# An adaLN block on one core: modulation products untied from the zero products, and a new written order

## The chip, the cores and the metric

The kernel runs on one core of one Trainium2 chip. The core has five engines with a queue each: TensorE (PE; its weight loads are shown apart as PEld), VectorE (DVE), ScalarE (ACT), GpSimd (POOL), and SyncE (SP), which here only issues DMAs. Each works off its own list of instructions in order and waits at semaphores for the others. The metric is the device time of one execution in microseconds (us), the median of several runs. A time, a start or an end without further words is in us from the start of the profiled span.

## What is computed

A transformer block with adaptive layer norm, for one sequence of 2048 tokens of width 640, in bf16:

```python
mod = (silu(c) @ w_mod).reshape(1, 6, 1, -1)
sa, ca, ga, sb, cb, gb = (mod[:, i] for i in range(6))
h = layernorm(x) * (1 + ca) + sa
q, k, v = split(h @ wqkv)                 # 32 heads of width 20
scores = q @ k^T * 20 ** -0.5             # causal, a window of 256 keys
x = x + ga * ((softmax(scores) @ v) @ wo)
h = layernorm(x) * (1 + cb) + sb
x = x + gb * ((sigmoid(h @ w_gate) * (h @ w_up)) @ w_down)   # inner width 1536
```

`silu(c) @ w_mod` gives the six modulation vectors. The first two, `sa` and `ca`, are needed before anything can be projected to q, k and v.

## The kernel before

**Order.** `build` does not issue instructions. It makes a list of 2021 operations (`A(...)`, that is `Prog.op`), each with the engines that may run it, what it reads and writes, and the tiles it occupies. `Prog.schedule` then walks through `PLAN`, a list of 2021 numbers written out by hand or by a search outside the file. A number `code` means: operation `code // 5` comes next, on engine `code % 5` of (pe, act, dve, pool, sp). So `PLAN` settles both the engine of an operation that has a choice and the order on each engine. `SLOTS` gives, in the order in which tiles are first used, which buffer of its pool each tile takes. Between engines nothing is ordered by `PLAN` itself: `Prog.emit` puts semaphore waits where an operation reads what another wrote, or takes a buffer that another has to leave. One more rule is in `schedule`: a POOL operation that stands in `PLAN` behind a DVE operation marked `port=True` waits for the last such one to end.

**Work.** The tokens go in 8 chunks of 256 (two blocks of 128 each). For a chunk: the layer norm statistics on DVE, a power on POOL, the normalised x on DVE or POOL, a transposition (on PE for chunks 0 and 1, by DMA later), the modulation by `sa` and `ca`, the projections, scores in sets of one PSUM tile S with an exponential on ACT (80 in all), masks on POOL, the product with v on PE ("pvs", two for each chunk), a normalisation on DVE, the output projection, the second norm and the gated MLP. As there is one S tile, a set of scores waits until the exponential of the set before has read it. The rest of PE's work is put between the sets.

**The start.** This is the part that the change names. Operation numbers are those of the kernel before.

- SP loads x of chunk 1 (27), the second half of chunk 0 (17), its first half (16), five pieces of `w_mod` for `sa` and `ca` (18 to 22, into the tile `wd`, which is free then), then wq, wk and so on.
- `zeros(n)` makes one PE operation of n products of a zero tile (each 128x512, into a bank of S that nobody reads). `HEAT` makes seven such operations (41 to 47, 11 products) ahead of the modulation products. `REHEAT` makes one after each of the five modulation operations: 51, 53, 55, 57 and 59.
- The modulation of the first norm, `fnA`: five operations on PE (50, 52, 54, 56, 58, called modA), one for each 128 rows of `w_mod`, of ten products of 64 columns each. Each has `extra=wprev`, that is, it also depends on the `zeros` operation made before it, and each `zeros` depends on the modA before it. So the twelve stand in one fixed order in any `PLAN`. A DVE copy (60) then brings the result to the tile mA, which every modulation of the first norm reads.
- Norm of chunk 0: statistics 67 to 69 (first half of the rows) and 70 to 72 (second half), powers 73 to 76 on POOL, normalised halves 77 and 78 on DVE, transpositions 79, 81 (of 77) and 88, 90 (of 78) on PE, copies out of PSUM 80, 82, 89, 91, modulations 83 to 87 and 92 to 96. Chunk 1: statistics 149 to 154, powers 155 and 156, normalised halves 157 and 158, transpositions 159 to 167.
- The first projections of q are 120 and 121, which read 92 to 96. The first set of scores is 308.

**Later operations that are spoken of.** 225 is the second group of modulation products ("modt"), which needs the last piece of `w_mod` (load 34, issued by SP). 220 to 224 scale `wo`, 370 to 381 scale `wd` by a gate vector ("wos", "wds"; DVE or POOL). 558, 645, 792 and 875 are the pvs of chunks 1 (first, second) and 2 (first, second). 303 to 307 are modulations of chunk 3's hT, 300 is a normalised half of chunk 3 on POOL.

**Lines of the profile.** L621 zero products, L634 full-array products (all projections, MLP, transpositions and modA), L635 products in parts of the array (scores, pvs, modt), L741 and L743 statistics, L747 and L749 powers, L762 and L759 normalised x, L726 the copy to mA, L822 and L823 modulations of chunk 0, L947 masks, L981 exponentials, L1206 wds, L1272 wos, L533 loads, L664 and L665 copies out of PSUM.

## Time and profile before

| | us |
|---|---|
| median of 3 runs (lowest, highest) | 324.32 (324.31, 324.38) |
| the profiled execution's own time | 324.32 |
| its span, first to last instruction | 322.6 |
| outside the span | 1.7 |
| PE busy | 316.8 |
| ACT, DVE, POOL busy | 214.6, 199.9, 193.9 |

A row of the timeline begins with the start in us, then the duration in us, the engine, the line, the operation, the tile it writes and the tile it reads, and the number of instructions merged into the row. In brackets stands the idle time of that engine just before and what ended it. Rows of grouped lines end with the busy time, the mean duration of one instruction in ns, and the idle time before the group. PE's products overlap, so the rate is read from the starts of many (15 products of 320 columns take 2.14 us), not from the duration of one.

### The profile page before, as it was taken

Reading aid. Unit: us, or ns where it says so; the run is one execution under the profiler, and the core shown is the slowest. Engines: PE = TensorE matmul, PEld = TensorE weight load, DVE = VectorE, ACT = ScalarE, POOL = GpSimd, SP = SyncE. Lnnn points to the kernel's source line nnn. Section 1 sums busy time; section 2 is a strip of 40 time slices with the busy share of each in tenths; the row PEclk is TensorE's granted clock in tenths of the full one; section 3 lists DMA queues with packets and bytes.
Section 4 is the critical chain, followed back from the end, with each engine's and each line's share of the span. In section 5 each row is a group of like instructions: output and inputs, shape, how many; then the busy total and the mean of one; then the engine's idle time right before and its main releaser. Section 6 shows DMA issues by size and latency. Waiting matters only on the chain.

```text
span 322.6 us, 11139 instructions
## 1 busy us (share of the span) xinstructions
PE 316.8 (98%) x4766; PEld 230.9 (72%) x4766; DVE 199.9 (62%) x424; ACT 214.6 (67%) x220; POOL 193.9 (60%) x334
## 2 busy tenths in 40 slices
PE   6999999999999999999999999999999999999997
PEld 2666656577776677766787667876788777877885
DVE  6796999677585545685557454676438453485422
ACT  1489999997798787859785858684768557200320
POOL 4338679788788596969393839585672836601000
PEclk9999999999999999999999999999999999999999
DMA  7999799999912343308250211420400021012111
GB/s 231 374 332 199 198 258 206 184 273 317 210 40 41 103 92 48 62 3 130 55 114 4 35 35 48 102 43 2 122 6 4 2 43 43 2 41 43 41 43 42
DMA packets 64619, 33.61 MB, mean 104 GB/s; under 512 B 49082, under 2 KB 63034, under 8 KB 64570
## 3 DMA queue, kind: packets, MB, share of 16 engines
q1 hardware_dynamic: 63744, 31.92, 42.3%
q10 hardware_dynamic: 826, 0.98, 0.9%
q8 instruction: 37, 0.61, 0.8%
q14 instruction: 12, 0.10, 0.1%
HBM read 18.35 MB, written 2.62 MB: 65 GB/s over the span
## 4 chain that ended last, share of the span: by engine, by line
PE 89%; POOL 4%; ACT 3%; DVE 2%; DMA 1%; issue 1%; SPq 0%; ACTq 0%; DVEq 0%; POOLq 0%
PE M L634 74%; PE S L635 8%; PE M L635 7%; POOL E L947 3%; ACT E L981 2%; DMA x<-in_A_x_dram 1%; DVE x L762 1%; DVE st L741 1%; POOL st L749 1%; POOL st L747 0%; ACT QT L664 0%; DVE hT L823 0%; DVE st L743 0%; ACT hT L777 0%; SPq L533 0%
## 5 line engine op out<-in xcount | busy, mean ns | idle before, releaser
L947 POOL TENSOR_SCALAR_AFFINE_SELECT E<-E 128x256 bf16<-128x256 bf16 (+2 forms) x234 | 149.3, 667 | 52.2 <-ACT E L981 34.5
L981 ACT ACTIVATE E<-S 128x2048 bf16<-128x2048 f32 x80 | 150.2, 1878 | 42.3 <-PE S L635 41.6
L634 PE MATMUL M<-h2T,wu 128*128 128x256 bf16 x480 | 66.4, 273 | 0.0
L634 PE MATMUL M<-h2T,wg 128*128 128x256 bf16 x480 | 65.8, 273 | 0.0
L1225 DVE SCALAR_TENSOR_TENSOR hh<-sig,M 128x512 bf16<-128x512 f32 x48 | 32.4, 681 | 43.8 <-ACT sig L1223 31.6
L634 PE MATMUL M<-wd,hh 128*128 128x320 bf16 (+2 forms) x396 | 56.4, 295 | 0.0
L634 PEld LDWEIGHTS M<-h2T,wu 128*128 128x128 bf16 x480 | 45.7, 98 | 8.1 <-issue 1.6
L634 PEld LDWEIGHTS M<-h2T,wg 128*128 128x128 bf16 x480 | 45.5, 98 | 8.3 <-issue 1.5
L634 PEld LDWEIGHTS M<-wd,hh 128*128 128x128 bf16 x396 | 37.0, 98 | 14.9 <-issue 1.4
L1223 ACT ACTIVATE sig<-M 128x512 f32<-128x512 f32 x48 | 28.4, 596 | 26.1 <-PE M L634 25.0
L635 PE MATMUL S<-QT,KT 20*64 20x64 bf16 (+5 forms) x1600 | 33.3, 231 | 0.5
L1112 DVE STREAM_TRANSPOSE T<-M 128x512 f32<-128x512 f32 x32 | 21.7, 698 | 12.2 <-PE S L635 10.0
L741 DVE BATCH_NORM_STATS2 st<-x 128x6 f32<-128x320 bf16 x64 | 28.3, 477 | 1.1 <-DMA x<-in_A_x_dram 0.8
L635 PEld LDWEIGHTS S<-QT,KT 20*64 20x64 bf16 (+1 forms) x1600 | 15.2, 99 | 18.4 <-ACT E L981 9.8
L634 PE MATMUL M<-wk,hT 128*128 128x320 bf16 x160 | 28.2, 300 | 0.0
L634 PE MATMUL M<-wv,hT 128*128 128x320 bf16 x160 | 28.0, 300 | 0.0
L634 PE MATMUL M<-wo,oT 128*128 128x320 bf16 x160 | 26.5, 300 | 0.0
L634 PE MATMUL M<-wq,hT 128*128 128x320 bf16 x160 | 26.0, 300 | 0.2 <-DVE hT L823 0.2
L1244 DVE TENSOR_TENSOR x<-M,x 128x320 bf16<-128x320 f32 (+2 forms) x33 | 15.4, 478 | 15.1 <-PE M L634 14.5
L1179 DVE TENSOR_TENSOR x<-M,x 128x320 bf16<-128x320 f32 x32 | 15.3, 487 | 13.6 <-PE M L634 13.0
L747 POOL TENSOR_SCALAR st<-st 128x2 f32<-128x2 f32 (+1 forms) x17 | 4.0, 233 | 32.7 <-DVE st L743 31.7
L635 PEld LDWEIGHTS M<-E,V 128*32 128x32 bf16 x960 | 19.9, 97 | 4.5 <-issue 2.2
(81 smaller groups left out, 298.9 us busy)
## 6 DMA issues: line engine op xcount, KB each, us to landing
x<-in_A_x_dram SPq DMA_DIRECT2D x11, 320.0 KB, 3.6
wd<-in_w_mod_dram SPq DMA_DIRECT2D x6, 320.0 KB, 5.0
wd<-in_B_w_down_dram SPq DMA_DIRECT2D x4, 480.0 KB, 5.3
out_dram<-x SPq DMA_DIRECT2D x5, 320.0 KB, 2.6
wg<-in_B_w_gate_dram SPq DMA_DIRECT2D x2, 576.0 KB, 6.9
wu<-in_B_w_up_dram SPq DMA_DIRECT2D x2, 576.0 KB, 6.2
wu<-in_w_mod_dram SPq DMA_DIRECT2D x1, 960.0 KB, 10.5
wq<-in_A_wqkv_dram SPq DMA_DIRECT2D x2, 400.0 KB, 6.7
```

What stands on the lines that cost most here:

```text
L634: return e.matmul(o, l, r, start=st, stop=sp, skip_group_check=True)
L635: return e.matmul(o, l, r, start=st, stop=sp, tile_position=tp, skip_group_check=True)
L741: A("dve", lambda e, g, bi=bi, j=j: e.bn_stats(v(bi * 12 + j * 6, 6), src[bi].ap[:, j * 320:(j + 1) * 320]), 0.48, reads=[src[bi].r()], wr ...
L747: A("pool", lambda e, g, lo=lo, w=w: e.tensor_scalar(v(28 + lo, w), var()[:, lo:lo + w], EPS, None, op0=ALU.add), 0.2, reads=[st.r(("m", b ...
L749: A("pool", lambda e, g, lo=lo, w=w: e.tensor_tensor(v(30 + lo, w), v(28 + lo, w), mhalf[:, 0:w], op=ALU.pow), 0.71, reads=[st.r(("v", lo) ...
L947: return lambda e, eng: e.affine_select(dst(), src(), pattern=pattern, compare_op=ALU.is_ge, fill=0.0, base=base, channel_multiplier=mul)
L981: A("act", lambda e, eng: e.activation(dst(), src(Sp.ap), ACT.Exp, scale=SM_SCALE), 1.876, reads=[Sp.r()], writes=[E.r()], prio=3, tag=f"e ...
L1112: A("dve", lambda e, g, h=h: e.transpose(T1.ap[:, 512 * h:512 * h + 512], X[h].ap), 0.694, reads=[X[h].r()], writes=[T1.r(h)], prio=3.5, t ...
L1179: A("dve", lambda e, g, ps=ps, bi=bi, half=half: e.tensor_tensor(x1[bi].ap[:, half * 320:half * 320 + 320], ps.ap[:, 0:320], x1[bi].ap[:, ...
L1223: A("act", lambda e, g, pg=pg, sg=sg: e.activation(sg.ap[:], pg.ap[:], ACT.Tanh, scale=0.5), c_act(512), reads=[pg.r()], writes=[sg.r()], ...
L1225: A("dve", lambda e, g, pu=pu, sg=sg, f0=f0: e.scalar_tensor_tensor(out=hh.ap[:, f0:f0 + 2, :], in0=sg.ap[:].rearrange("p (a b) -> p a b", ...
L1244: A("dve", lambda e, g, ps=ps, bi=bi, c0=c0, n=n: e.tensor_tensor(x1[bi].ap[:, c0:c0 + n], ps.ap[:, 0:n], x1[bi].ap[:, c0:c0 + n], op=ALU. ...
```

## The change

Three things. First, the modulation products no longer depend on `zeros` operations (`extra=wprev` is gone), so an order may put them elsewhere among the zero products. Second, `REHEAT` becomes (2, 1, 1, 0, 3): there is one `zeros` operation less (57), while the number of zero products stays 18, the one of 57 being issued by 59. Third, `PLAN` and `SLOTS` are new: 2020 numbers, the first 150 places searched anew and the others moved a little.

```diff
-REHEAT = (2, 1, 1, 1, 2)
+REHEAT = (2, 1, 1, 0, 3)
...
         if kt:
-            zeros(REHEAT[kt - 1], oA[-1:])
-        oA.append(A("pe", fnA, MW / 2400.0 * 10, reads=[Rm[0][kt], R_silubc], writes=[psA.r()], prio=0, lat=0.2, tag="modA", extra=wprev))
+            if REHEAT[kt - 1]:
+                zeros(REHEAT[kt - 1], oA[-1:])
+        oA.append(A("pe", fnA, MW / 2400.0 * 10, reads=[Rm[0][kt], R_silubc], writes=[psA.r()], prio=0, lat=0.2, tag="modA"))
```

The beginning of the old and the new `PLAN`:

```diff
-    76, 139, 89, 63, 84, 202, 94, 3, 8, 243, 38, 175, 245, 72, 182, 186, 192, 197, 99, 53, 58, 13, 33, 18, 48, 104,
-    109, 114, 357, 352, 124, 119, 129, 134, 747, 362, 378, 383, 337, 342, 392, 767, 347, 752, 762, 205, 210, 215,
...
+    243, 3, 8, 33, 76, 48, 28, 245, 38, 175, 58, 23, 202, 182, 139, 757, 205, 210, 215, 220, 225, 230, 89, 84, 94,
+    63, 186, 192, 197, 99, 332, 104, 13, 337, 342, 109, 352, 363, 347, 250, 260, 742, 368, 357, 373, 382, 400, 235,
```

Read out by engine, with the numbers of the kernel before (in the new file every operation from 58 on has a number smaller by one), the start is:

```
PE before: 35 49 41-46 88 47 90 50 51 52 53 81 54 79 55 56 57 58 59 159 167 161 120 121 163 ...
PE after:  49 35 41-46 50 52 81 47 51 79 53 54 55 88 90 56 58 59 159 161 167 120 121 163 ...
DVE before: 40 14 36 38 39 71 70 149 72 67 68 78 153 69 150 152 154 151 77 89 82 158 157 60 96 92 94 95 ...
DVE after:  40 36 152 38 39 67 68 69 71 70 149 72 77 153 150 154 151 78 158 157 60 93 96 95 168 14 85 ...
POOL before: ... 75 76 73 74 155 156 86 84 239 ...
POOL after:  ... 73 74 75 76 155 156 92 13 83 84 86 3 10 239 ...
ACT before: 15 37 91 80 93 160 162 87 ...
ACT after:  15 37 82 80 91 89 94 160 87 162 164 ...
```

SP issues the same loads in the same order up to load 29 of the modulation weights. Behind the start, 109 operations have another engine: 33 went from ACT to DVE, 31 from DVE to ACT, 27 from DVE or ACT to POOL, 12 from POOL to DVE or ACT, and 6 DMA issues between SP and ACT. The places that matter below:

```
POOL before, up to the masks of 558: ... 297 298 299 300 247 327 330 then 12 masks
POOL after,  up to the masks of 558: ... 297 298 299 245 249 327 330 300 224 221 223 then 12 masks, 307 and 305 among them
PE before: 554 342 272 278 279 282 558 474 475 471 225 566 ...
PE after:  554 278 282 279 225 558 474 475 471 486 472 499 566 ...
ACT before, between the exponentials of 554 and 558: 305 306 304 303 307
ACT after,  between the exponentials of 554 and 558: 280 215 303
POOL before, from the masks of 645 to those of 875: 24 masks, 5 wds, 2 bmodu0, 2 xh5, 4 pow5, 2 bpow1
POOL after,  from the masks of 645 to those of 875: 24 masks, 6 wds, 2 bmodu0, 2 xh5, 1 pow5, 2 pow6, 1 amodu5
```

Ahead of 792, PE does 12 steps of the MLP of chunk 0 less than before (two products of 256 columns each), and ahead of 875 it does 6 steps of k projections and 3 of the down projection less; these follow behind.

14 lines of the change are left out of this document (7 added, 7 removed), and 216 rows, old and new, of the table PLAN.

## The prediction

> **What bounds the kernel now.** I read the page first (busy shares, then the chain that ended last), then the windows by stage, then the timeline of the start and of the places where PE waits.
>
> ```profile
> PE 316.8 (98%) x4766; PEld 230.9 (72%) x4766; DVE 199.9 (62%) x424; ACT 214.6 (67%) x220; POOL 193.9 (60%) x334
> ...
> PE 89%; POOL 4%; ACT 3%; DVE 2%; DMA 1%; issue 1%; SPq 0%; ACTq 0%; DVEq 0%; POOLq 0%
> ```
>
> PE is busy for 316.8 of 322.6 us and holds 89% of the chain. It works off one list, and every projection, score and MLP product of the old list is in the new one. So the time can move in two ways only: the first useful product starts earlier or later, or PE waits more or less afterwards. The first is set by this stretch:
>
> ```profile
> 3.13 0.49 DVE L609 COPY silubc<-siluc 128x320 bf16<-128x320 bf16 x1
> ...
> 4.41 1.28 DVE L741 BATCH_NORM_STATS2 st<-x 128x6 f32<-128x320 bf16 x3 [0.78 <-DMA x<-in_A_x_dram]
> ...
> 5.88 0.23 POOL L747 TENSOR_SCALAR st<-st 128x1 f32<-128x1 f32 x1 [2.41 <-DVE st L743]
> 5.90 0.89 DVE L741 BATCH_NORM_STATS2 st<-x 128x6 f32<-128x320 bf16 x2
> ...
> 6.20 0.58 POOL L749 TENSOR_TENSOR st<-st,mhalf 128x1 f32<-128x1 f32 x1
> 6.82 0.45 DVE L762 TENSOR_SCALAR x<-x,st 128x640 bf16<-128x640 bf16 x1
> ...
> 8.56 0.28 DVE L743 BATCH_NORM_AGGREGATE st<-st 128x2 f32<-128x12 f32 x2
> ...
> 9.64 0.71 POOL L749 TENSOR_TENSOR st<-st,mhalf 128x2 f32<-128x2 f32 x1
> ...
> 10.39 0.81 DVE L762 TENSOR_SCALAR x<-x,st 128x640 bf16<-128x640 bf16 x2 [0.36 <-POOL st L749]
> ...
> 11.10 0.17 DVE L726 COPY mA<-S 128x10 f32<-128x10 f32 x1
> ...
> 12.05 0.94 PE L634 MATMUL M<-wq,hT 128*128 128x320 bf16 x5 [0.24 <-DVE hT L823]
> ...
> 12.55 0.90 POOL L823 TENSOR_SCALAR hT<-hT,mA 128x128 bf16<-128x128 bf16 x2 [2.20 <-DVE hT L823]
> ```
>
> The reader is to see that DVE hardly pauses from 4.41 to 11.27: statistics, normalised halves, and only then the copy to mA. The first projection starts at 12.05, when the modulations behind that copy are through. The modulation products on PE are not late:
>
> ```profile
> 2.72 4.44 PE L621 MATMUL S<-E 128*128 128x512 bf16 x10
> ...
> 8.12 0.59 PE L621 MATMUL S<-E 128*128 128x512 bf16 x2
> ...
> 10.60 0.45 PE L634 MATMUL S<-silubc,wd 128*128 128x64 bf16 x10
> ```
>
> The last ten end at 11.05, just ahead of the copy at 11.10. So the dependency that is taken out costs little by itself; what counts is the new order.
>
> **The start, step by step.** The new DVE list takes the first half of chunk 0 (16) before the second (17). The loads are issued as before, and they land so:
>
> ```profile
> 1.30 0.45 SPq L533 DMA_DIRECT2D x<-in_A_x_dram  x1
> ...
> DMA to landing us min/median/max: 3.1/3.1/3.1
> ```
>
> ```profile
> 1.80 0.42 SPq L533 DMA_DIRECT2D x<-in_A_x_dram  x1
> ...
> DMA to landing us min/median/max: 4.1/4.1/4.1
> ```
>
> The second half is there at 1.30 + 3.1 = 4.4, the first only at 1.80 + 4.1 = 5.9. Before, DVE used the time between for the second half's three statistics (4.41). In the new list only 152, siluc (38) and silubc (39) stand ahead of 67. Chunk 1 was loaded first, so 152 is done by about 4.4 and silubc by about 5.1 (0.49, and a short step before it). DVE then stands still from 5.1 to 5.9. From there: 67 and 68 until 6.8 (0.89), 69 until 7.0, three statistics in 1.2 until 8.2, 72 until 8.4. The normalised half 77 runs 8.4 to 8.8 (its power on POOL is done at 8.0). Two statistics (0.8) and two aggregates (0.28) end at 9.8. The powers 155 and 156 follow at 9.9 and end at 9.9 + 0.32 + 0.71 = 10.95; 78 hides in that time. Then 158 and 157 take 0.81, and the copy to mA starts at about 11.7 and not at 11.10. PE is ready for it: 88 and 90 follow 78 at 10.3, 56 and 58 end by 11.4.
>
> ```profile
> 2.62 0.42 POOL L554 MEMSET stg<- 128x384 bf16 x1
> ```
>
> Behind the copy (11.87) the modulation 92 now goes to POOL: 0.1 to hand over and 0.45, so projection 120 starts at 12.45 instead of 12.05: **+0.4**. POOL has four operations behind it (13, 83, 84, 86: 0.42 + 3 x 0.45) and ends at 14.2; projection 98 wants 86 at 14.35. That cover is thin: one more modulation there would cost 0.3.
>
> From 12.05 to score set 308 both lists hold the same operations. The chain shows a pause ahead of that set:
>
> ```profile
> 18.80 0.14 issue
> ```
>
> The new list puts transposition 103 one step (two products) earlier, which covers the copy 104. So 308 is late by 0.4 - 0.15 = **+0.25**. Bounds of the start: -0.35, if the first half lands as fast as the second (DVE's pause of 0.8 gone: 0.4 - 0.8 and some 0.05 elsewhere), and +0.7, if the modulations on POOL come late as well. I take +0.25, which uses the landing as the row shows it.
>
> **At the first pvs of chunk 1 (558).** In the new list POOL gets three scalings of wo, one normalised half and two modulations between the last mask of chunk 0 and those of 558; PE gets modt (225) ahead of 558.
>
> ```profile
> 33.26 3.06 POOL L947 TENSOR_SCALAR_AFFINE_SELECT E<-E 128x1024 bf16<-128x1024 bf16 x2
> 39.29 1.22 POOL L947 TENSOR_SCALAR_AFFINE_SELECT E<-E 128x512 bf16<-128x512 bf16 x2 [2.97 <-DVE wo L1272]
> 42.21 5.66 POOL L947 TENSOR_SCALAR_AFFINE_SELECT E<-E 128x1024 bf16<-128x1024 bf16 x8 [1.70 <-ACT V L664]
> 48.21 2.13 POOL L947 TENSOR_SCALAR_AFFINE_SELECT E<-E 128x1024 bf16<-128x1024 bf16 x2 [0.34 <-ACT E L981]
> ```
>
> ```profile
> L1206 POOL TENSOR_TENSOR wd<-wd,gbc 128x640 bf16<-128x640 bf16 x5 | 6.9, 1394 | 1.8 <-DVE hT L778 1.2 <-DMA wd<-in_B_w_down_dram 0.5
> L759 POOL TENSOR_SCALAR x<-x,st 128x640 bf16<-128x640 bf16 x6 | 5.2, 871 | 1.6 <-PE M L634 1.2 <-POOL st L754 0.2 <-DVE Tn L1116 0.2
> ...
> L778 POOL TENSOR_SCALAR hT<-hT,mA 128x256 bf16<-128x256 bf16 x5 | 2.8, 556 | 0.0
> ```
>
> ```profile
> 50.62 1.50 PE L635 MATMUL M<-E,V 128*32 128x256 bf16 x64
> ...
> 54.08 0.24 PE L635 MATMUL M<-hh,silubc 128*32 128x160 bf16 x4
> 54.44 0.40 PE L635 MATMUL S<-QT,KT 20*128 20x128 bf16 x16
> ```
>
> Before, POOL was free at 36.32, worked 9.0 on these masks (1.22 + 5.66 + 2.13) and idled 5.0 (2.97 + 1.70 + 0.34). The added work is 3 x 1.39 (row of wd, same shape) + 0.87 + 2 x 0.56 = 6.2, more than the idle time. Without any idle POOL ends at 36.3 + 0.25 + 9.0 + 6.2 = 51.75. PE comes there at 50.62 + 0.25 + 0.7 (modt: ten groups of four products, some 0.07 apart) = 51.57. So PE waits **+0.2**, between 0 and 1 (if a fifth of the old idle time stays). Behind 558 something goes: the set at 54.44 waited for an exponential that ACT started late, because four modulations stood before it.
>
> ```profile
> 50.42 2.06 ACT L777 ACTIVATE hT<-hT,mA 128x256 bf16<-128x256 bf16 x4
> ```
>
> The new list has three shorter operations there (some 1.2), and modt is gone from the gap. The step from 54.08 to 54.44 should shrink to 0.07: **-0.29**. Load 34, which modt needs, now stands in SP's list behind a transposition that waits for q of chunk 2. I put its issue at 46.0 instead of 43.62:
>
> ```profile
> L533 SPq DMA_DIRECT2D hh<-in_w_mod_dram x1: 469/469/469, 43.6 to 43.6; - x1
> ...
> DMA to landing us min/median/max: 2.9/3.4/4.6
> ```
>
> With 2.9 to 4.6 it lands by 50.6, and modt starts at 50.9: just hidden, at most 0.4 if it is slower.
>
> **The rest.** The other 96 or so changed places trade copies and modulations between engines that are 60 to 67% busy. I count them as nothing, with +-0.3 for small waits. The tail (15 steps of the last down projection, a residual sum, an output) keeps its form. **Sum: 0.25 + 0.2 - 0.29 = +0.16.** The profiled execution took 324.32, its span 322.6 and 1.7 around it, and equals the median; so 324.48, rounded 324.5.
>
> **Rivals.**
>
> *Faster (323.4).* The first half lands at 4.9 or earlier in other runs, so the start gains 0.35 instead of losing 0.25, and the two waits of PE that rows show later (0.29 above, 0.24 below) both go: 324.32 - 0.35 - 0.53 = 323.4. For it: ACT's list holds 82 operations up to 875 where it held 90, and exponentials come earlier. Against it: the landing stands in the trace, and POOL gets fuller.
>
> *Slower: POOL becomes the bound ahead of the second pvs of chunk 2 (875).*
>
> ```profile
> 68.00:88.00 20.00, 20.00 (x251) 14.76 (x247) 14.18 (x27) 16.39 (x19) 16.04 (x22) 1.00 1.09 275
> 88.00:106.00 18.00, 17.76 (x272) 12.11 (x264) 12.47 (x30) 15.02 (x15) 15.65 (x20) 1.00 0.25 58
> ```
>
> ```profile
> 105.34 1.50 PE L635 MATMUL M<-E,V 128*32 128x256 bf16 x64 [0.24 <-POOL E L947]
> ```
>
> ```profile
> 24.10 2.15 PE M L634 x15
> ```
>
> Here the fifth pair of numbers is POOL: 31.7 busy of 38, 6.3 idle, and PE still waited 0.24 for a mask. In the new list PE comes to 875 with 15 products of k and 12 of the down projection less, at 0.143 each (15 in 2.15) 3.85 earlier, and POOL has one wd scaling and one modulation more and three small ones less, +0.65. Of 6.3 only 1.8 may stay idle. Half of it, 3.15, would make PE wait 1.35: 324.5 + 1.35 - 0.24 = 325.6. It decides above 1.8. Against it: the exponentials, whose ends POOL waits for, come earlier too.
>
> *Slower: PE falls back to half rate in the start (326.7).* In the new list PE has nothing from about 8.1 (50 and 52 done) to 8.9 (77 done). The ten zero products at 2.72 took 0.44 each, two at 8.12 together 0.59, a step of about 0.21 between them: PE changes its rate near 7.1. If the pause undid that, PE's work from 81 to 58 (2.5 at full rate) would take 2.5 more, less 0.3 of slack: +2.2. No pause like it is in the trace. The Trainium skill, "TensorE: Matmul & The Clock Gate", section "Part 1: The HAM clock gate", says that the clock is halved until about 3.4 us of sustained work and falls back only after an idle window of about that length. The trace agrees with the first half (4.4 us of slow products); by the second half this rival would not occur, and the sum would stay as it is.
>
> That the change doesn't do what it says is part of the forecast: 18 zero products stay 18, and the freed products end behind the DVE work anyway.
>
> **Chances.** Runs of this kernel tell 0.2%, 0.65 us, from no change: 323.67 to 324.97. Forecast 0.41 (own range 323.7 to 325.0), the faster case 0.30, POOL at 875 0.25, half rate 0.04. So faster 0.30, same 0.41, slower 0.29. The range reaches from 323.2, a little below the faster case, to 325.9, a little above POOL's; the half rate and longer waits lie outside.
>
> **What would show it.** Right: the first statistics of chunk 0 start at 5.9 behind a DVE pause; the copy to mA at about 11.7; the first projection near 12.45; set 308 near 19.2; PE waiting for a mask at 558 near 51.7; no gap behind 558. Wrong: a copy to mA before 11.1 (the landing or the DVE sum is wrong), a wait of PE over 0.5 ahead of 875 (POOL), zero products 0.43 apart after 9 us (the rate), or a PE wait at modt for its load.

## The result, and the profile after

The changed kernel takes 330.46 us (median of 6 runs, 330.15 to 330.80), the kernel before 324.66 beside it (6 runs): the ratio is 1.0166, interval 1.0135 to 1.0196. The prediction was 324.5, range 323.2 to 325.9. So the time is 5.8 us above the kernel before and 4.6 us above the top of the range, on the side to which the prediction gave 0.29.

The page of the profiled execution after (330.37 us, span 328.3), its busy line and the chain by engine:

```profile
PE 318.1 (97%) x4765; PEld 230.6 (70%) x4766; DVE 205.5 (63%) x421; ACT 208.5 (64%) x208; POOL 207.4 (63%) x349
...
PE 87%; DVE 8%; issue 2%; DMA 1%; ACT 1%; POOL 0%; SPq 0%; DVEq 0%; POOLq 0%
```

The chain has changed its second engine: DVE holds 8% where it held 2, and POOL 0 where it held 4. DVE is busy 5.6 us longer with three instructions fewer. It is not that it was given more work: with the mean duration that each kind of DVE instruction (operation, tile and shape) had before, the new list would be 1.8 us shorter. The same kinds took 6.8 us longer in all, above all x (2.8), hT (2.3), Tn (1.4) and wo (1.2).

First the start, on which most of the prediction's working was spent. Timeline after, DVE and PE:

```profile
5.61 0.89 DVE L742 BATCH_NORM_STATS2 st<-x 128x6 f32<-128x320 bf16 x2 [0.52 <-DMA x<-in_A_x_dram]
...
11.29 0.16 DVE L727 COPY mA<-S 128x10 f32<-128x10 f32 x1
```

```profile
12.21 1.06 PE L634 MATMUL M<-wq,hT 128*128 128x320 bf16 x5 [0.19 <-POOL hT L824]
...
18.96 0.40 PE L635 MATMUL S<-QT,KT 20*128 20x256 bf16 x8
```

The first set of scores starts at 18.96 (18.94 before). In this execution the start, which the change names, has cost nothing. Now the same walk for the starts of the pvs: 558 at 50.62 before and 54.61 after, where 0.7 is modt, pulled ahead; 645 at 67.05 and 71.33; 875 at 105.34 and 107.19, where the new order has 3.85 us less for PE ahead of it (by the prediction's sum), so the delay is 5.7; the last result at 320.39 and 325.95. The loss arises between 33 and 70 us (some 4.3) and between 97 and 106 (some 1.5), and stays the same from there to the end. The windows of those two stretches, before and after (sums of busy time for PE, PEld, DVE, ACT and POOL in this order):

```profile
33.00:52.00 19.00, 18.84 (x268) 11.72 (x266) 18.10 (x42) 18.24 (x21) 13.71 (x19) 1.00 0.93 235
97.00:110.00 13.00, 12.76 (x236) 8.38 (x235) 8.07 (x23) 9.99 (x11) 9.48 (x17) 1.00 0.30 77
```

```profile
33.00:52.00 19.00, 16.52 (x190) 9.42 (x188) 18.32 (x33) 14.40 (x14) 18.06 (x19) 1.00 0.98 239
97.00:110.00 13.00, 11.70 (x203) 7.96 (x202) 9.51 (x18) 9.76 (x10) 10.84 (x13) 1.00 0.15 28
```

From 33 to 52 DVE was busy 18.10 of 19 us before, with 42 instructions (or merged pieces); after, it is busy 18.32 with 33. POOL went from 13.71 to 18.06. DVE had no slack in this stretch even before, whatever its 62% over the span. PE's own waits in these stretches (rows of PE's timeline after with a bracket of 0.5 us or more behind 33 us):

```profile
35.75 0.40 PE L635 MATMUL S<-QT,KT 20*128 20x256 bf16 x8 [1.02 <-DMA KT<-stg]
...
43.88 0.85 PE L634 MATMUL M<-wq,hT 128*128 128x320 bf16 x5 [1.31 <-DVE stg L665]
...
68.41 0.45 PE L634 MATMUL M<-grow,ident 128*128 128x160 bf16 x4 [0.83 <-DVE V L665]
...
101.58 1.80 PE L634 MATMUL M<-wd,hh 128*128 128x320 bf16 x12 [0.78 <-DVE hh L1226]
...
103.91 0.72 PE L634 MATMUL M<-wd,hh 128*128 128x320 bf16 x4 [0.52 <-DVE hh L1226]
```

Four of the five waits are for DVE: copies out of PSUM (stg, V), of which PE needs the buffer, and hh. All five add up to 4.5 us; measured by the starts of the products, over their usual step, each is some 0.1 longer (1.09, 1.48, 0.99, 0.84, 0.69). With the small ones, PE pauses behind 11.5 us come to some 5.4 us more than before by the starts (the figure moves by a few tenths with what is taken for the usual step), nearly the whole loss of the profiled execution (the spans differ by 5.7). What was DVE doing? Its timeline after, and POOL's over the same time:

```profile
34.99 1.64 DVE L763 TENSOR_SCALAR x<-x,st 128x640 bf16<-128x640 bf16 x1
...
37.29 0.82 DVE L779 TENSOR_SCALAR hT<-hT,mA 128x256 bf16<-128x256 bf16 x1
38.03 0.48 DVE L665 CAST V<-M 128x320 bf16<-128x320 f32 x1
...
40.15 1.28 DVE L1117 TENSOR_TENSOR Tn<-T,Dr 128x640 bf16<-128x640 f32 x1
41.35 1.68 DVE L1273 TENSOR_TENSOR wo<-wo,gbc 128x640 bf16<-128x640 bf16 x1
...
43.36 0.47 DVE L665 CAST stg<-M 128x320 bf16<-128x320 f32 x1
```

```profile
33.40 3.06 POOL L948 TENSOR_SCALAR_AFFINE_SELECT E<-E 128x1024 bf16<-128x1024 bf16 x2
36.44 1.59 POOL L760 TENSOR_SCALAR x<-x,st 128x640 bf16<-128x640 bf16 x1
38.00 4.68 POOL L1273 TENSOR_TENSOR wo<-wo,gbc 128x640 bf16<-128x640 bf16 x3
```

Read the two together. The x of 34.99 takes 1.64 us and ends at 36.63, just behind POOL's masks (33.40 to 36.46); the same instruction took 0.43 before. The Tn of 40.15 (1.28) and the wo of 41.35 (1.68) lie beside POOL's three wos of 38.00 to 42.68; they took 0.82 and 0.43 before. POOL is stopped as well: its x of 36.44 took 1.59 beside DVE's Tn and hT in place of 0.87. The copies out of PSUM (0.47, 0.48) between them are as short as ever. By groups, DVE from 33 to 52 us, before and after (count, busy us, mean ns):

```profile
L1272 DVE TENSOR_TENSOR wo<-wo,gbc 128x640 bf16<-128x640 bf16 x5 | 2.7, 564 | 0.0
...
L1116 DVE TENSOR_TENSOR Tn<-T,Dr 128x640 bf16<-128x640 f32 x2 | 1.6, 816 | 0.0
...
L762 DVE TENSOR_SCALAR x<-x,st 128x640 bf16<-128x640 bf16 x1 | 0.4, 435 | 0.0
```

```profile
L1273 DVE TENSOR_TENSOR wo<-wo,gbc 128x640 bf16<-128x640 bf16 x2 | 2.3, 1168 | 0.0
L665 DVE CAST V<-M 128x320 bf16<-128x320 f32 x5 | 2.3, 459 | 0.0
...
L1117 DVE TENSOR_TENSOR Tn<-T,Dr 128x640 bf16<-128x640 f32 x2 | 2.1, 1048 | 0.0
L779 DVE TENSOR_SCALAR hT<-hT,mA 128x256 bf16<-128x256 bf16 x2 | 1.7, 873 | 0.0
```

Two wos cost DVE 2.3 us, where five cost it 2.7. Taking three of the five off DVE and giving them to POOL freed 0.4 us of DVE and no more. In the second stretch DVE is not full by the window (9.51 of 13), but DVE works without a pause from 94.7 to 103.9. Among this work are four wd of 0.75 us each and two x of 0.94, and hh stands behind them.

This gave the theory that the experiments were to test: **DVE and POOL can't both work on SBUF tiles at a time, POOL's new work stands beside DVE's operations of that kind, and DVE, full in that stretch, is late with what PE waits for.** The rivals: the start and the untied products; DVE's own order and number of operations; late loads and transpositions.

### The profile page after: what moved, and what is told of

Its sections match the earlier page's. It is cut to its first block, busy times and chain, and to the rows that moved or that the text cites. A ratio compares the mean times of both kernels' runs of the same rounds, so it can differ in the third digit from the quotient of the medians.

```text
span 328.3 us, 11139 instructions
## 1 busy us (share of the span) xinstructions
PE 318.1 (97%) x4765; PEld 230.6 (70%) x4766; DVE 205.5 (63%) x421; ACT 208.5 (64%) x208; POOL 207.4 (63%) x349
## 3 DMA queue, kind: packets, MB, share of 16 engines
q10 hardware_dynamic: 1370, 1.64, 1.6%
## 4 chain that ended last, share of the span: by engine, by line
PE 87%; DVE 8%; issue 2%; DMA 1%; ACT 1%; POOL 0%; SPq 0%; DVEq 0%; POOLq 0%
PE M L634 72%; PE S L635 8%; PE M L635 7%; DVE st L742 2%; DMA x<-in_A_x_dram 1%; DVE x L763 1%; DVE V L665 1%; DVE T L1113 1%; DVE stg L665 1%; ACT E L982 1%; DVE hT L779 1%; DVE Tn L1117 0%; DVE KT L665 0%; SPq L533 0%; DVE st L744 0%
## 5 line engine op out<-in xcount | busy, mean ns | idle before, releaser
L1226 DVE SCALAR_TENSOR_TENSOR hh<-sig,M 128x512 bf16<-128x512 f32 x48 | 32.4, 681 | 49.5 <-ACT sig L1224 35.0
L634 PEld LDWEIGHTS M<-h2T,wg 128*128 128x128 bf16 x480 | 46.5, 98 | 6.9 <-issue 0.7
L634 PEld LDWEIGHTS M<-h2T,wu 128*128 128x128 bf16 x480 | 44.7, 98 | 9.3 <-issue 3.5
L634 PE MATMUL M<-wk,hT 128*128 128x320 bf16 x160 | 26.9, 300 | 0.0
L634 PE MATMUL M<-wv,hT 128*128 128x320 bf16 x160 | 26.3, 300 | 0.0
L634 PE MATMUL M<-wo,oT 128*128 128x320 bf16 x160 | 25.8, 300 | 0.1
L635 PE MATMUL M<-E,V 128*32 128x256 bf16 (+1 forms) x960 | 22.7, 246 | 0.0
```

Of the source, the lines that this page charges most:

```text
L634: return e.matmul(o, l, r, start=st, stop=sp, skip_group_check=True)
L635: return e.matmul(o, l, r, start=st, stop=sp, tile_position=tp, skip_group_check=True)
L1226: A("dve", lambda e, g, pu=pu, sg=sg, f0=f0: e.scalar_tensor_tensor(out=hh.ap[:, f0:f0 + 2, :], in0=sg.ap[:].rearrange("p (a b) -> p a b", ...
```

## The experiments

The names: "places" are places of `PLAN`; in the lists of places of the changed kernel, code = 5 x (number - 1) + engine for operations from 58 on. The kernel before ran beside each group, with medians from 324.66 to 325.73 over the groups; ratios are to these.

### Where the loss is: three orders put together

```diff
-PLAN = AFTER
+PLAN = AFTER[:150] + [c for c in BEFORE if c // 5 not in {d // 5 for d in AFTER[:150]}]    # start_only
+PLAN = AFTER[:610] + [c for c in BEFORE if c // 5 not in {d // 5 for d in AFTER[:610]}]    # early_only
+PLAN = BEFORE[:610] + [c for c in AFTER if c // 5 not in {d // 5 for d in BEFORE[:610]}]   # late_only
```

(`BEFORE` in the numbers of the new file; the buffers of the tiles taken as in the two lists, and another free one where that was taken.)

> The changed kernel's first 150 places (untied products, one zero product operation less, new start), then every other operation in the order, and on the engine, that the kernel before gave it. Theory (the time is lost behind the start, where POOL's new work and DVE's stand in each other's way): 324.3 to 324.9, within 0.2% of before. Rival (the start and the untied products lose it): 329 to 331, like the changed kernel.

> The changed kernel's first 610 places (all up to about 85 us), then the rest as before. Theory (about 4.3 us are lost between 33 and 70 us, about 1.5 between 97 and 108, nothing behind): 328.5 to 329.3, before plus 4.3. Rival (the places behind 110 us lose much of it): under 327.

> The other way round: the first 610 places as before, then the rest in the changed kernel's order. Theory: only the loss at 97 to 108 us is left, 325.8 to 326.4, before plus 1.5. Rival (the losses are no property of the two places, and come back wherever DVE is short): over 328.

start_only: 325.74 us, ratio 1.0026 (1.0003 to 1.0048). early_only: 330.70, ratio 1.0191 (1.0143 to 1.0238). late_only: 328.60, ratio 1.0114 (1.0068 to 1.0160).

The start with the untied products costs 0.3%, not 1.7%; the rival of the start falls, though 325.74 is 0.8 above what was expected of it. In its trace the first set of scores starts at 18.62, earlier than before; the time goes in a wait of 1.02 at 33, of which below, and one of 0.50 for hh at 80. early_only is 1.4 us above the top of its range and late_only 2.2; by the number alone late_only's rival was right. Their traces show why the two don't add up. Both have waits that neither parent has, where the two orders are joined, near 88 us (in early_only 0.85 for a copy on ACT at 89.2 and 1.11 for a residual sum on DVE at 91.2), and in late_only the waits at 101 and 103 don't occur at all. PE's timeline of late_only:

```profile
88.26 1.50 PE L630 MATMUL M<-E,V 128*32 128x256 bf16 x64 [2.13 <-POOL E L943]
```

Without its seam early_only carries the waits of the changed kernel at 35, 43 and 68 (1.03, 1.32, 0.82), which is where the theory put them. One thing was new: start_only and late_only, whose order at 33 us is the old one, wait there 1.02 and 1.18 us for a transposition of Q, and before's profile has no such wait. This is the last question below.

### Is it POOL's work? Shortened masks

The mask of a block of scores is written by POOL. Here it covers 4 columns of each 128; instructions, order and waits stay.

```diff
-ap = lambda E=E, st=st: E.ap[:].rearrange(...)[:, :, 0:128]
-mask(a, 16 // st * 128, select(ap, ap, [[0, 16 // st], [1, 128]], 0, -1), ...)
+ap = lambda E=E, st=st: E.ap[:].rearrange(...)[:, :, 0:4]
+mask(a, 16 // st * 128, select(ap, ap, [[0, 16 // st], [1, 4]], 0, -1), ...)
```

> The changed kernel with the masks of chunks 0, 1 and 2 working on 4 of each 128 columns (the rest of their part of the computation is left out): same instructions, order and waits, but POOL is done with each in about 0.1 to 0.2 us in place of 0.6 to 1.5. Theory (DVE's operations from one SBUF tile to another can't run while POOL works on SBUF, so DVE is late with the copies that PE waits for): the x of 1.64 us at 35 and of 0.94 at 99, and wd of 0.75, go back to 0.43 to 0.5, the waits of PE at 42, 67, 100 and 103 (1.48, 0.99, 0.84, 0.69 us) shrink by 2 to 4 us together: 326.4 to 328.4. The wait of about 1.1 for K at 34 stays. Rival (DVE is late there by its own order and number of operations): 329.6 to 330.5.

> The same shortened masks (the rest of their part of the computation left out) in the kernel before. Theory: PE has nothing to gain there, its waits behind DVE are small: 323.6 to 324.9. Rival (shorter masks are worth the same in any order): 2 us or more below before.

short_after: 326.65 us, ratio 1.0064 (1.0041 to 1.0087), 3.8 us below the changed kernel (1.0% by the two ratios, 3.3 us: the two ran in different groups). short_before: 324.29, ratio 0.9983 (0.9959 to 1.0006), no change. The same edit is worth 3.8 us in one order and 0.7 by the medians, with an interval that reaches over no change, in the other. The x of 35 us is back at 0.44; at 98 us x, Tn and hh have their usual lengths and PE waits for nothing.

Which stretch is it? Shorten the masks of chunk 2 alone (`4 if a == 2 else 128`), and in the other direction add the last POOL work that short_after left in the first stretch, the wos:

```diff
-A(WSE[0], lambda e, g, t=t: e.tensor_tensor(wo[:, t, :], wo[:, t, :], gbc[:], op=ALU.mult), WS, port=True,
+w = 8 if t in (1, 3, 4) else D
+A(WSE[0], lambda e, g, t=t, w=w: e.tensor_tensor(wo[:, t, 0:w], wo[:, t, 0:w], gbc[:, 0:w], op=ALU.mult), WS, port=True,
```

> The changed kernel with only the masks of chunk 2 (those of 73 to 106 us) on 4 of each 128 columns, the rest of their part left out. Theory: the waits for hh at 100.6 and 103 (0.84 and 0.69 us) go, those at 42 and 67 stay: 328.6 to 329.3. Rival (what short_after gained comes from POOL running early in general, and not from the places of the collisions): no change at 100, 330 to 330.6.

> short_after (masks of chunks 0 to 2 on 4 of each 128 columns, the rest of their part of the computation left out), and the three scalings of wo on POOL on 8 of 640 columns (the rest left out too). Theory (POOL's work on SBUF stops DVE, whatever it is): the wait of 0.66 us for a copy of V at 38.2, the one that short_after kept in that stretch, goes to 0.2 or less, DVE's Tn there back to 0.8: 325.7 to 326.3, with only the wait for K at 34 left of the loss. Rival (the scalings do not matter): 326.5 to 326.8, the level of short_after.

short_late: 329.00 us, ratio 1.0109 (1.0084 to 1.0135). short_wos: 326.23, ratio 1.0019 (1.0005 to 1.0033). Windows of short_late behind 97 us:

```profile
97.00:110.00 13.00, 13.00 (x215) 9.11 (x212) 7.99 (x20) 10.91 (x10) 4.37 (x13) 1.00 0.34 47
```

PE is full there (13.00 in place of 11.70), DVE needs 7.99 in place of 9.51, and its waits at 43 and 68 are as before this edit. So the second stretch is made by the masks that stand in it, and costs some 1.5 us (330.46 - 329.00; 1.8 by the ratios). In short_wos PE waits for nothing between 36 and 50, and DVE's row of 35.5 us, which short_after had at 2.02 beside POOL's wos, reads:

```profile
35.53 0.82 DVE L1117 TENSOR_TENSOR Tn<-T,Dr 128x640 bf16<-128x640 f32 x1
```

What is left is the wait for K at 35 (0.97 there), and 0.2% by the ratio. Each edit leaves the order, the engines and the number of instructions as they are, so the list as such is not what loses the time; POOL's work beside it is.

### The same from the other side: POOL work added to the kernel before

```diff
+pad = sb("pad", [128, D])
...
+for _ in range(4):
+    A("pool", lambda e, g: e.tensor_tensor(pad[:, 320:640], pad[:, 0:320], pad[:, 0:320], op=ALU.mult), 0.7, ...)
...
-    2670, 1653, 1012, 1122,
+    2670, 1653, 10113, 10118, 10123, 10128, 1012, 1122,
```

> The kernel before plus four POOL products of two tiles on a buffer of their own (320 columns, some 0.7 us each alone), put in POOL's order where it idles 2.97 us at 36.3; nothing reads them, so nothing can be late by its data. Theory (POOL at work on SBUF stops DVE's operations from SBUF to SBUF): DVE's wo, Tn, x of 36.6 to 40.5 us (0.45, 0.81, 0.43 each) get longer by 1.5 to 3 us together, DVE's copies come later, PE waits for them between 38 and 45, and the time is 325.5 to 327. Rival (POOL's own lateness is what costs): the idle time takes them up, 324.3 to 325.

before_pads: 326.72 us, ratio 1.0040 (1.0019 to 1.0062). The time fell into the interval, but only half of it for the reason given. DVE's groups from 33 to 52 us:

```profile
L1112 DVE TENSOR_TENSOR Tn<-T,Dr 128x640 bf16<-128x640 f32 x2 | 2.2, 1078 | 0.0
...
L758 DVE TENSOR_SCALAR x<-x,st 128x640 bf16<-128x640 bf16 x1 | 0.8, 840 | 0.0
```

Tn went from 816 to 1078 ns on the mean and x from 435 to 840, from four products that nothing reads: 0.9 us longer together, against 1.5 to 3 expected. The wos did not get longer (2.5 us in place of 2.7): the first of them, 0.93 before, had been stopped by masks in the kernel before already. PE waited 0.26 at 40.7 and 0.28 at 42.1 behind DVE's transpositions T (some 0.8 together by the starts of its products), where before has no such row. The other 1.4 is the wait for Q at 33 again. So the direction is shown, and the size is smaller than expected, since DVE met the added work with few operations of the kind.

### The exclusion by itself

Six DVE operations of a kind, alone and then beside six of POOL, the two started together:

```diff
+stages = [(None, p) for p in (p_mask, p_wo, p_x)] + [(d, None) for d in D] + [(d, p_mask) for d in D]
+stages += [(d_x, p_wo), (d_Tn, p_wo), (d_x, p_x), (d_cast, p_wo)]
```

> None of the block is computed (the input is copied to the output). Six DVE operations of a kind at a time, first alone, then beside six POOL masks of 128x512: normalised x (640 columns, bf16), a scaling of wo (two bf16 tiles), a modulation (256 columns), the quotient Tn (two f32 tiles in, bf16 out), a copy out of PSUM, and statistics. Theory: alone 0.43, 0.43, 0.33, 0.81, 0.47 and 0.47 us each as in before; beside the masks the first four take 0.8 us or more on the mean, since they and the masks run one after the other, the copies and the statistics stay within 10%. Rival (DVE and POOL share nothing that matters): all six stay.

Its timeline. POOL's masks and products alone, then DVE's x (L32), wo (L35), hT (L38), Tn (L41), copy (L46) and statistics (L49) alone, then the same six beside masks, then x and Tn beside POOL products:

```profile
6.26 3.58 POOL L53 TENSOR_SCALAR_AFFINE_SELECT m<-E 128x512 bf16<-128x512 bf16 x6 [0.17 <-POOL pdst L82]
9.99 8.14 POOL L56 TENSOR_TENSOR pdst<-psrc 128x640 bf16<-128x640 bf16 x6
...
23.73 2.23 DVE L32 TENSOR_SCALAR dst<-src,st 128x640 bf16<-128x640 bf16 x6 [19.74 <-POOL pdst L59]
26.06 2.50 DVE L35 TENSOR_TENSOR dst<-src 128x640 bf16<-128x640 bf16 x6
28.67 1.63 DVE L38 TENSOR_SCALAR dst<-src,st 128x256 bf16<-128x256 bf16 x6
30.40 4.50 DVE L41 TENSOR_TENSOR dst<-T,Dr 128x640 bf16<-128x640 f32 x6
35.01 2.48 DVE L46 CAST dst<-M 128x320 bf16<-128x320 f32 x6
37.59 2.46 DVE L49 BATCH_NORM_STATS2 bn<-src 128x6 f32<-128x320 bf16 x6
40.16 3.80 DVE L32 TENSOR_SCALAR dst<-src,st 128x640 bf16<-128x640 bf16 x6
...
44.49 4.68 DVE L35 TENSOR_TENSOR dst<-src 128x640 bf16<-128x640 bf16 x6 [0.53 <-POOL m L53]
49.70 3.75 DVE L38 TENSOR_SCALAR dst<-src,st 128x256 bf16<-128x256 bf16 x6 [0.53 <-POOL m L53]
53.55 7.13 DVE L41 TENSOR_TENSOR dst<-T,Dr 128x640 bf16<-128x640 f32 x6
...
60.79 2.48 DVE L46 CAST dst<-M 128x320 bf16<-128x320 f32 x6
64.37 2.46 DVE L49 BATCH_NORM_STATS2 bn<-src 128x6 f32<-128x320 bf16 x6 [1.10 <-POOL m L53]
68.08 7.61 DVE L32 TENSOR_SCALAR dst<-src,st 128x640 bf16<-128x640 bf16 x6 [1.25 <-POOL m L53]
...
76.97 10.49 DVE L41 TENSOR_TENSOR dst<-T,Dr 128x640 bf16<-128x640 f32 x6 [1.28 <-POOL pdst L56]
```

Beside masks that take 3.58 us alone, x needs 1.57 us more, wo 2.18, hT 2.12 and Tn 2.63; the copy and the statistics not a hundredth. By the mean duration of one, in which the 0.8 was meant, wo (0.84) and Tn (1.25) met it, x (0.70) and hT (0.69) missed it. Beside POOL products of 8.14 us, x needs 5.38 more and Tn 5.99, and a copy nothing; beside POOL's own normalised x (5.17 alone), x needs 2.11 more. So here one us of POOL's work costs DVE 0.4 to 0.75 us, as long as DVE has such operations to do.

The single instructions show the two taking turns: each DVE x behind the first ends 0.17 or 0.18 us behind one of POOL's masks, as the x of 34.99 did in the changed kernel (36.63 and 36.46). POOL pays too: a mask of 0.64 us alone takes 0.73 on the mean beside x, 0.88 beside wo and 1.12 beside Tn. Not the whole of an instruction excludes the other: x and masks need 2.23 + 3.58 = 5.8 us alone and 4.3 together, and beside hT the masks lose nothing.

### What doesn't help: moving single operations in the changed kernel

wos_dve gives the three wos back to DVE; casts_first puts what PE waits for ahead of long operations in DVE's list; copies_act gives eight copies to ACT.

```diff
-    1056, 1118, 1103, 1025, 1113, 2645, ... 1672, 1107, ... 1275, 1097,        # wos_dve
+    1056, 1117, 1025, 2645, ... 1672, 1112, 1107, ... 1275, 1102, 1097,
...
-    1672, 1107, 1271, ... 2525, 1792, 1787, 2517,                              # casts_first
+    1672, 1271, ... 1302, 1107, 1245, ... 2532, 1792, 1787, 2965,
...
-    1037, ... 1302, ... 1007, ... 1257, ... 1442, ... 2467, ... 2517, ... 2547,  # copies_act
+    1036, ... 1301, ... 1006, ... 1256, ... 1441, ... 2466, ... 2516, ... 2546,
```

> The changed kernel with only its three scalings of wo (224, 221, 223) taken from POOL back to DVE. Theory (POOL's operations on bf16 tiles lengthen DVE's beside them, and DVE is then late with copies out of PSUM): 328.4 to 329.6, a gain of 0.8 to 2 us, with the normalised x at 35 us still long beside the masks, but the quotient Tn of 1.28 us back at about 0.8 and the wo of 1.68 us at 0.45 to 0.9. Rival (DVE has too much work there, and the three are a relief): 330.8 to 332, as DVE gets 1.3 us more work. Rival (the late transpositions of K alone, their order on SP): 330.4, no change.

> The changed kernel with only DVE's order changed at three places, so that what PE waits for stands ahead of long operations from SBUF to SBUF: wo 222 behind the copy 261 (at 41), the x of 358 and 359 behind the copies of V 504, 510, 507 (at 66), the x of 865 and 866, and their transposition 867, behind the product hh 441 (at 99). Engines, POOL and PE as in the changed kernel. Theory (PE waits because the copies are queued behind operations that POOL stops): the waits of 1.48 at 42, 0.99 at 67 and 0.84 and 0.69 at 101 and 103 shrink by 2 to 3.5 us together: 327 to 328.4. Rival (PE waits for POOL's masks or for loads): 330 to 330.6.

> The changed kernel with eight copies out of PSUM (208, 261, 202, 252, 289 of 36 to 50 us, 494, 504, 510 of 62 to 68) taken from DVE to ACT at their places in the order. DVE is busy 18.3 of the 19 us from 33 to 52, ACT 14.4. Theory (DVE, its operations lengthened by POOL's, is the bound of this stretch, so that moving one wait only makes another, as in wos_dve and casts_first; only less work on DVE helps): the waits between 38 and 52 and the one at 67 shrink by 1.5 to 2.5 us together, 328 to 329.2. Rival (the copies are as late on ACT, behind exponentials of 1.88 us each): 330 to 331.

wos_dve: 330.51 us, ratio 1.0171 (1.0138 to 1.0204). casts_first: 330.43, ratio 1.0140 (1.0115 to 1.0165). copies_act: 335.03, ratio 1.0297 (1.0264 to 1.0330). Three misses, and of use. The time of wos_dve is that of its last rival, and the time of casts_first that of its only one, but not for their reasons: in both the wait for K is the same (0.93 and 1.01), and all other waits of PE are still for DVE, at other places. The collision only changes partners. DVE's timeline, beside the masks at 34 to 37 and POOL's x at 37:

```profile
35.73 1.61 DVE L1268 TENSOR_TENSOR wo<-wo,gbc 128x640 bf16<-128x640 bf16 x1
37.27 0.43 DVE L758 TENSOR_SCALAR x<-x,st 128x640 bf16<-128x640 bf16 x1
37.62 1.33 DVE L1112 TENSOR_TENSOR Tn<-T,Dr 128x640 bf16<-128x640 f32 x1
```

Now wo stands where x stood and is stopped in its place, x is short, and PE waits 1.02 for a copy of V at 40 and 0.61 for oT at 47 in place of 1.31 for stg at 44. casts_first did what it set out to do at 44 (the copy came 1.8 us earlier), and then PE waited 0.75 for oT at 45.8, 1.08 for a copy of gbc at 69.4, and in one pause of 1.4 at 102 for what had been two: DVE works through the same list with the same stops, and something is always last. So, as far as these two orders show, it matters less where in DVE's list the urgent copy stands than how long the whole list takes. copies_act shows the limit of giving work away one by one: the copies stand behind exponentials of 1.88 us in ACT's list, and PE waited 2.40 for one of V at 41, 1.22 for stg at 51 and 1.33 for another of V at 73.

> The changed kernel's order throughout, but behind its first 150 places each operation on the engine that it had before (95 operations go back; POOL loses some 13 us of work). Theory: what collides is set by both, the order and the engines; with POOL's wos, x and modulations back on DVE and ACT the collisions at 42 go, but the order still puts masks beside the x, Tn and wd of 35, 66 and 97: 326.5 to 328.5. Rival 1 (the moved engines are all of it): 324.5 to 325.5. Rival 2 (the order is all of it): 330 or more.

> The other way round: the order, the start and the zero products of the kernel before, with the changed kernel's engines behind place 150. Theory (both): 325.5 to 328, with DVE's x, Tn or wo beside POOL's wos longer than in before, and PE waiting for DVE's copies between 36 and 50. Rival 1 (the engines are all of it): 329 or more. Rival 2 (the order is all of it): 324.2 to 325.

```diff
-PLAN = AFTER
+PLAN = [c if k < 150 else c // 5 * 5 + engine_before[c // 5] for k, c in enumerate(AFTER)]    # engines_before
-PLAN = BEFORE
+PLAN = [c if k < 150 else c // 5 * 5 + engine_after[c // 5] for k, c in enumerate(BEFORE)]    # engines_after
```

engines_before: 368.68 us, ratio 1.1352 (1.1317 to 1.1387). engines_after: 357.05, ratio 1.0976 (1.0955 to 1.0996). (Of the 109 operations that the change puts on other engines, 14 stand within the first 150 places, so 95 are moved here.) No theory came near, and the pair tells nothing about which of the two, order or engines, made the collisions: PE has new waits in both, up to 5.7 us for a copy of V on ACT and 4.9 for a wd on POOL in engines_before, and 7.7 in all for masks in engines_after. Part of the time is the clock: PE's granted clock is 0.97 and 0.99 of full speed on the mean (0.82 from 33 to 52 us in engines_before), where all runs above have 1.0 or nearly so. A likely reading is that an operation put on another engine, at a place that was found for the first one, holds up what stands behind it; neither run isolates that. In this kernel an order and its engines could not be exchanged one by one.

### The wait at 33: transpositions of Q and K

> The kernel before with each of its 18 zero products of 512 columns replaced by two of 256: the same time on PE, 36 instructions more. In before a block of PE's instructions (16 KB, 256 of them, so 7.7 us of PE here) is fetched at 32.45 us, as the transposition of the second half of Q (issued 29.79) has nearly landed (32.9); 36 instructions more bring the block to about 31.4. Theory (a block fetched into the transpositions of Q and K delays their landing by over a microsecond, and the first set of scores of chunk 1 waits for it; that is what start_only lost at 33.16): this transposition takes about 4.5 us in place of 3.1, PE waits 0.9 to 1.2 us at 33, and the time is 325.2 to 326.0. Rival (the landing is late for another reason, as the earlier start of the transpositions): no wait there, 324.2 to 324.9.

> start_only with each zero product of 512 columns made four of 128: the same columns, 108 instructions more, so the block of PE's instructions that was fetched at 31.59 in start_only comes about 3.3 us earlier, near 28.3, ahead of the transposition of the second half of Q (issued 29.79). Theory (the block in the transpositions costs the wait at 33): the wait of 1.09 us goes to 0.3 or less, and the time is 324.2 to 324.9, 0.8 to 1.4 below start_only, perhaps below before. Rival (the block only has to fall anywhere on the transpositions): the wait stays at about 1, 325.2 to 326.

> start_only with one load of wo (480 KB, issued by SP at 24.75 us, ahead of the transpositions of Q and K of chunk 1) issued some 10 us earlier, behind load 29. Theory (what delays these transpositions is other traffic of the DMA engines among them, a load and PE's instruction block): the first two land about 1 us sooner, the wait of 1.09 at 33 goes to 0.4 or less, 324.4 to 325.2, the level of before. Rival (the instruction block alone): the wait stays at 0.9 to 1.1, 325.3 to 326.

> The kernel before with the one load of wo that SP issues at 25.05 us, ahead of the transpositions of Q and K of chunk 1, issued behind load 29 instead, some 11 us earlier. Theory (traffic among the transpositions delays them in some executions of before too, and with them the first scores of chunk 1): the lowest times stay at 324.2 to 324.4, but more of the executions are there, so that the median is 0.3 to 0.9 below that of the runs of before beside it. Rival (the instruction block alone delays them): the same median within 0.2.

```diff
-for k in range(n):
-    ins = e.matmul(p_S.aps[0][:, 3, :], Eall[:, 0, 0:128], Eall[:, 0, 128:640], start=True, stop=True)
+for k in range(2 * n):        # halves_before; in start_quarters 4 * n, 0:128 and 128:256
+    ins = e.matmul(p_S.aps[0][:, 3, 0:256], Eall[:, 0, 0:128], Eall[:, 0, 128:384], start=True, stop=True)
...
-    149, 169, ... 1467, 164, 901,        # before_wo; start_wo alike
+    149, 164, 169, ... 1467, 901,
```

halves_before: 325.57 us, ratio 1.0018 (1.0002 to 1.0033). start_quarters: 326.79, ratio 1.0038 (1.0017 to 1.0060). start_wo: 325.20, ratio 0.9987 (0.9969 to 1.0004). before_wo: 324.87, ratio 0.9995 (0.9982 to 1.0009).

The last transposition of Q that the scores at 33 need took 3.1 us from issue to landing in before, short_before and before_wo, and 4.2 to 4.9 in start_only, late_only, halves_before, start_quarters, start_wo and before_pads. What is beside it shows in the DMA rows from 31.4 to 32.4 us, of before and of start_only (each digit is the time of the packets that start in one of 40 slices, as a share of the 16 DMA engines; before has no instruction queue in this stretch):

```profile
DMA  9999999999599999999999999999988999999652
```

```profile
DMA  9999999999999599990000000000000000000000
...
q8 instruction: 1, 0.02, 5.8%
```

In start_only a block of 16 KB of instructions comes as one packet of 0.93 us at 31.59. In the last 0.55 us of the row no packet starts: packets of the transpositions that started just behind the block took up to 1.69 us each, where 0.02 is usual. halves_before, which changes nothing but the number of PE's instructions, has such a block at 31.66 (31.4 expected) and a landing of 4.5 (4.5 expected), yet the wait was 0.50 and not 0.9 to 1.2, as PE had already lost 0.3 to a load of wk; another 0.7 of its profiled time is a wait for hh at 217, of which nothing was foreseen. In start_quarters the block did not move as expected (31.59 again), so that kernel tells nothing for or against it. Its time is a start that was 0.7 later and a wait of 0.82 for a load of w_gate at 84; the pause at 34 is only 0.29 by the starts, as PE came there later. start_wo brought the first two transpositions to 3.1 and 3.2 us (4.5 and 5.6 in start_only), as expected of a load taken away, but the third, with a block at 32.02, still took 4.7, and PE waited 0.48; the time is at the top of the theory's interval. In before_wo the rival was right: the median is the same, though the longest of 12 runs is 325.64 against 326.16.

So the wait of 1.0 us at 35 in the changed kernel is no collision of DVE and POOL: it is 0.99 in short_after and 0.97 in short_wos, where POOL's long operations of that stretch are gone. Nor does it come and go, as that for Q does. In all eight traces with the changed order at this place (after, early_only, short_after, short_late, short_wos, wos_dve, casts_first, copies_act) the K transposition takes 4.9 to 5.0 us and the wait is 0.93 to 1.03.

Does the block make both waits? Its place against the end of the landing doesn't tell. It comes in the last 0.45 us of the three short landings, 0.65 to 1.7 us ahead of where 3.1 would have ended in five of the long ones of Q, but only 0.1 to 0.2 us ahead of it for K in those eight, and 0.3 in before_pads (4.9). The starts of the transpositions' packets fit better. In the three short landings at most one packet starts behind the block before the next transposition is issued. In the five long ones of Q and the eight of K, over 100 still start behind it (for K a second transposition was issued 1.3 us behind the first), then hardly any for 1.25 us (at most 35 in each quarter of a us, mostly under 10, where about 200 is usual). before_pads doesn't fit that either, as nothing is left to start when its block comes. No run moved the block and nothing else by a known step, so it isn't settled; nor is why the changed order always meets one at K.

No kernel here that computes the whole block beats the one before. start_wo and before_wo reach it.

## Why the prediction was wrong

**The start: right mechanism, size off, as bounded.** DVE did stand still ahead of the first statistics, 0.52 and not 0.8, since the half landed at 5.58 (3.78 after its issue; 4.1 was taken). They began at 5.61 (5.9 predicted), the copy to mA at 11.29 (11.7), the first projection at 12.21 (12.45), set 308 at 18.96 (19.2). The term +0.25 was +0.02, inside its bounds; with the same start, start_only had set 308 at 18.62, so a few tenths of it move from one execution to the next.

**At 558: the wrong engine.** The working filled POOL up (ends 51.75) and compared it with PE (51.57). PE came to 558 at 54.61 and did not wait for a mask there. POOL was indeed full, as worked out, and done with the masks only at 54.25, because its own operations were stopped too (x 1.59 us in place of 0.87, the third wo 1.98 where 1.39 was taken) and it idled 1.05 for an exponential. But PE was later still, by way of DVE, which is no term of that sum.

**Behind 558: right.** From 54.61 to 56.05 to 56.38 there is no pause, the 0.29 is gone.

**The rest: the step that failed.** "The other 96 or so changed places trade copies and modulations between engines that are 60 to 67% busy. I count them as nothing, with +-0.3 for small waits." Two things are wrong with it. The 60 to 67% are means over the span, and from 33 to 52 us DVE was 18.10 of 19 busy: work that gets longer there has nowhere to go. And POOL's added work, 6.2 us by the prediction's own sum, was priced as POOL's time alone. At 0.4 to 0.75 us of DVE for each us of POOL (alone_and_beside) it is worth, as an estimate, 2.5 to 4.6 us of DVE, where DVE has operations between SBUF tiles to do. What the runs put in its place, by the medians: some 1.5 us at 97 to 106 (short_late), some 2.4 more between 33 and 70 (3.8 in short_after less 1.5), 0.4 of the wos (short_wos), and about 1.0 of the wait for K, which no edit took away and whose cause is open: 5.3 of 5.8. The runs of before in the three groups have medians up to 1.1 apart, so a single share is good to about a us. What they say together is firmer: with POOL's masks and wos cut short the ratio falls from 1.0166 to 1.0019.

None of the signs that the prediction named for being wrong occurred: the copy to mA came at 11.29, PE did not wait for POOL ahead of 875, the zero products behind 9 us ran at full rate, and modt did not wait for its load. The loss came by a way for which it had no term and no sign.

The trace of before had a hint of it. Its own POOL idled 2.97 us at 36.32, "<-DVE wo", by the rule in `schedule` that POOL waits for the last DVE operation with `port=True`. The name of that mark, and the prediction's own row with that bracket, suggested that the two get in each other's way, and the wo of 35.73 us, 0.93 beside masks where the next ones took 0.43, showed it once; the prediction read the idle time as room to fill. The rule guards one side only: nothing keeps DVE from running into a POOL operation that started first.

**The rivals.** PE's rate in the start held: three zero products at 8.43 took 0.81 together. POOL as the bound ahead of 875 did not occur: PE waited for DVE's hh there, and POOL's share of the chain went to 0. Both rivals looked at engines one by one, and the loss lay between two. The chance of slower, 0.29, rested on the wrong mechanism, and the range ended where that mechanism ended.

## What to carry to other kernels

Before work is moved to an idle engine, look at what it does to the engines that are full in the same stretch, in windows of that stretch and not by shares of the span. Where DVE is full, a us of GpSimd work on SBUF tiles can cost it half a us or more (0.4 to 0.75 here). A group that keeps its shape and grows in mean duration from one trace to the next (wo: 564 to 1168 ns) is the sign of it, and moving the victims about in the list only picked other victims here.

## What the runs showed of the hardware

DVE and POOL stop each other, instruction by instruction, on some operations only: DVE's bf16 tensor by scalar and its products of two SBUF tiles go from 0.37, 0.42, 0.27 and 0.75 us each (x, wo, hT, Tn; a sixth of the time of six in a row) to 0.63, 0.78, 0.63 and 1.19 beside masks, and x to 1.27 beside POOL products; copies out of PSUM and statistics stay at 0.41. POOL's masks go from 0.64 us each to as much as 1.12 in turn. The Trainium skill, "SBUF — State Buffer", section "Who interferes with whom", states that DVE's second pair of ports is shared with GpSimd as an exclusive lock, taken for a whole instruction by whoever issues first, and that it concerns DVE's two-port modes and DVE instructions with two SBUF inputs. The traces agree in which operations are hit (wo and Tn have two SBUF inputs; that x and hT run in a two-port mode no run here shows) and in that the one waits for the other's end (the x of 34.99 us waits out the mask that began at 34.45 and ended at 36.45). They differ in one point: some of each instruction overlaps the other's (4.3 us for x and masks that need 5.8 alone). The price per us of POOL's work is the runs' own.

A block of PE's instructions on its way from memory seems to hold up a transposition whose packets are still starting: landings of 3.1 us in the three traces where they had all started, and 4.2 to 5.0 in the thirteen where over 100 had not; before_pads, with 4.9, is the exception named above. The Trainium skill, "Runtime: NRT & Kernel Launch", section "Instruction fetch mechanics", says that instructions come in 16 KiB blocks over a DMA queue and that the cost of crossing a boundary is mostly hidden. The size agrees (37 packets and 0.61 MB on q8 in the page of after); if the reading above is right, the cost was not hidden here, as it fell on another transfer and not on the engine that fetched. This also bears on measuring: the kernel before itself ran from 324.18 to 326.98 us in these groups, and an edit that only moves the number of instructions (halves_before) was worth 0.2%.
